# One factor for the second softmax's sum and the RMS norm, taken from turned squares

## The chip, the core and the metric

The kernel runs on one core of a Trainium2 chip. A core has TensorE (PE in the profile) for matrix products, VectorE (DVE), ScalarE (ACT), GpSimd (POOL), and a queue engine SP that issues the DMAs. The metric is the device time of one launch in microseconds (us).

## The reference, cut to what matters

Two softmax attentions come first, for 8 batches, 8 heads, 576 tokens and a head dimension of 64; 32 packed queries per head gather the tokens, and the tokens then read the packed rows back:

```
p_packed = sm_attn(p, k, v)                # 32 rows a head
out      = sm_attn(q, p_packed, p_packed)  # 576 tokens, softmax over 32 weights
x        = out, 8 heads side by side       # 4608 tokens x 512
xn       = x / sqrt(mean(x*x) + 1e-6) * rms_g
h        = silu(xn @ w_gate) * (xn @ w_val)
```

Four products with further weights follow (`w_out`, `w1`, `w2`, `w3`, `w_out2`). The change touches the second softmax and the RMS norm.

## The kernel before, in words

The kernel never forms `x`. It multiplies the packed rows with the gate and value weights (`wb_unit`, L383 to L397), and a dense stage multiplies that with the second softmax's weights of one batch, laid out as `ah` and `al`, the two halves of a split float32 (`split`, L58: ScalarE writes the high part, VectorE subtracts). `ah[:, e]` and `al[:, e]` exist for e = 0 and 1, four heads each.

`dense_units` (L418) runs over 8 batches and 6 column groups; each pair makes 8 units of six 288-column products. One unit after the other, even units (gate) are read by ScalarE's tanh (L438) and then VectorE (L439, "th"), odd ones (value) by ScalarE's copy (L447) and GpSimd (L448); in batch 0 VectorE does that last step (L444). Four PSUM banks hold the units, so unit n+4 can't start before unit n has been read. The six products of a unit take, in order, `ah` 0, `ah` 1, `al` 0, `al` 1, `ah` 0, `ah` 1. After units 3, 11, 19, 27, 35 and 43 of a batch stands the next `wb_unit`: one product (L391), a ScalarE copy (`wbh`) and a VectorE subtraction (`wbl`).

All engines run their instructions in program order, and the order is written out by hand. `unpack(b)` (L284) is a generator of 18 steps, `pack(b)` (L202) one of 7, and `ow` converts weights (two ScalarE, two VectorE, one GpSimd instruction each). `planned` (L490) takes a step of a generator after a unit: `UNPACK`, `PACK` and `WOUT` hold, for the batches 2 to 6, the unit within the batch (0 to 47) after which each step is issued; `PLAN` does so for batches 0 and 1 (units 0 to 95), and a string of letters for the prologue (x is a filler product, p, u, P, U are steps of pack and unpack). While batch b runs in the dense stage, `unpack(b+1)` is issued between its units.

The 18 steps of `unpack` before, for a batch other than 0: 1 scores (L303) and VectorE's 32x32 transposes; 2 to 5 row maximum, subtraction, exp; 6 and 7 row sum, reciprocal `rs2`, and GpSimd's multiplication of `a2` by it (L322); 8 and 9 the transposes into `a2T` (L327), with a DMA that rotates half 1 into `turned`; 10 and 11 the product of `a2T` with the 32x32 Gram matrix `G` (L343) and the elementwise product `sq`; 12 GpSimd's addition of the two halves of `sq` (L352); 13 five products with a column of ones (L359), which sum over heads, and `ssq` (L361); 14 GpSimd's power of -0.5 (L364); 15 five TensorE transposes that spread the factor over all partitions (L369) and VectorE's multiplication of half 0 (L371); 16 the same multiplication for half 1; 17 and 18 the splits into `ah` and `al`. Small PSUM results use `slot("at")`, of which there are two.

Of the kernel before, what the change touches and what calls it, by code (L numbers as in the profile page):

```python
# [8 lines left out]
F32 = mybir.dt.float32  # L9
# [23 lines left out]
def packed_attention_swiglu_bilinear(ctx: ExitStack, tc, qT, kT, v, v_end, pT, rms_g, w_gv, w_out,  # L33
                                     w1, w2, w3T, w_out2, out):
    nc = tc.nc
# [16 lines left out]
    def slot(tag):  # L52
        return slots.tile([128, 2, 512], F32, tag=tag, name=tag, bufs=2)
# [15 lines left out]
    att = att_ctx.enter_context(tc.tile_pool(name="att", bufs=1, side="left"))  # L69
# [23 lines left out]
    def load_q(b):  # L93
        load("q", qT, b, 2)
# [90 lines left out]
    wgv = wraw.tile([128, NC, 2, DFF], F32, name="wgv")  # L185
    bdP1T = att.tile([128, 2, NC, 2, NP], F32, name="bdP1T")
    G = att.tile([128, 2, 2, NP], F32, name="G")
    mhalf = att.tile([128, R], F32, name="mhalf")
    ones = att.tile([128, 2], F32, name="ones")
    nc.gpsimd.memset(ones, 1.0 / DM)  # L190
    nc.scalar.activation(out=ones[:, 1:], in_=ones[:, :1], func=AF.Exp)
    nc.gpsimd.memset(ones, 1.0 / DM)
    nc.gpsimd.memset(mhalf, -0.5)
    nc.gpsimd.memset(bdP1T, 0.0)


# [2 lines left out]
    def place(c, e):  # L199
        return 32 * ((c + e) % NC)  # L200
# [80 lines left out]
    NB = S // 32  # L281


    def unpack(b):  # L284
        assert ("bd", b) in over
        qs = raw.pop(("q", b))
        a2 = att.tile([128, 2, NB, NP], F32, tag="a2", name="a2")
        mx2 = att.tile([128, 2, NB], F32, tag="mx2", name="mx2")
        rs2 = att.tile([128, 2, NB], F32, tag="rs2", name="rs2")

        def halves(x):
            return x.rearrange("p (a n) -> p a n", a=2)
# [13 lines left out]
        for a, t in enumerate(ts):
            nc.vector.transpose(out=a2.rearrange("p e t n -> p e (t n)")[:, :, HALF * a:HALF * a + HALF],
                                in_=t[:, :, :HALF])
        yield
        if b > 1:  # L310
            load_q(b + 2)
        for e in range(2):
            nc.vector.tensor_reduce(out=mx2[:, e], in_=a2[:, e], axis=AX.X, op=ALU.max)
            yield
            nc.vector.tensor_tensor(out=a2[:, e], in0=a2[:, e], in1=wide(mx2[:, e]), op=ALU.subtract)
            nc.scalar.activation(out=a2[:, e], in_=a2[:, e], func=AF.Exp, scale=SCALE)
            yield
        for e in range(2):
            nc.vector.tensor_reduce(out=rs2[:, e], in_=a2[:, e], axis=AX.X, op=ALU.add)
            nc.vector.tensor_scalar(out=rs2[:, e], in0=rs2[:, e], scalar1=1e-9, scalar2=None, op0=ALU.add)  # L320
            nc.vector.reciprocal(out=rs2[:, e], in_=rs2[:, e])
            nc.gpsimd.tensor_tensor(out=a2[:, e], in0=a2[:, e], in1=wide(rs2[:, e]), op=ALU.mult)  # L322
            yield
        a2T = att.tile([128, 2, S], F32, tag="a2T", name="a2T")
        order = (0, 1) if b == 0 else (1, 0)
        for e in order:
            nc.vector.transpose(out=a2T[:, e], in_=a2[:, e].rearrange("p t n -> p (t n)"))  # L327
            if b and e:
                turned = att.tile([128, S], F32, tag="turned", name="turned")
                nc.sync.dma_start(out=turned[:96], in_=a2T[32:, 1])  # L330
                nc.sync.dma_start(out=turned[96:], in_=a2T[:32, 1])
            yield

        assert ("made", b) in over
        sq = att.tile([128, 2, S], F32, tag="sq", name="sq")
        ts = [slot("at") for _ in range(2)]
        for a in range(2):
            for e in range(2):
                for c in range(NC):
                    r = place(c, e)  # L340
                    k = r if b == 0 else 32 * c
                    x = turned[k:k + 32] if b and e else a2T[k:k + 32, e]
                    nc.tensor.matmul(ts[e][r:r + 32, a, :HALF], lhsT=G[k:k + 32, b % 2, e],  # L343
                                     rhs=x[:, HALF * a:HALF * a + HALF],
                                     start=True, stop=True, tile_position=(k, r))
        over.add(("G", b))
        for e in range(2):
            nc.vector.tensor_tensor(out=halves(sq[:, e]), in0=ts[e][:, :, :HALF], in1=halves(a2T[:, e]),
                                    op=ALU.mult)
            yield  # L350
        if b:
            nc.gpsimd.tensor_tensor(out=sq[:, 0], in0=sq[:, 0], in1=sq[:, 1], op=ALU.add)  # L352
        yield
        ssq = att.tile([128, R], F32, tag="ssq", name="ssq")
        rinv = att.tile([128, R], F32, tag="rinv", name="rinv")
        t = slot("at")
        for r in range(R):
            for e in range(1 if b else 2):
                nc.tensor.matmul(t[:, 0, 2 * r:2 * r + 2], lhsT=sq[:, e, T0[r]:T0[r] + 128], rhs=ones,  # L359
                                 start=(e == 0), stop=(e == 1 or b > 0), skip_group_check=True)  # L360
        nc.vector.tensor_scalar(out=ssq, in0=t[:, 0, :2 * R].rearrange("p (r j) -> p r j", j=2)[:, :, 0],  # L361
                                scalar1=0.0, scalar2=1e-6, op0=ALU.max, op1=ALU.add)
        yield
        nc.gpsimd.tensor_tensor(out=rinv, in0=ssq, in1=mhalf, op=ALU.pow)  # L364
        yield

        t = slot("at").rearrange("p a n -> p (a n)")
        for r in range(R):
            nc.tensor.transpose(t[:, 64 + T0[r]:192 + T0[r]], rinv[:, r:r + 1].to_broadcast([128, 128]), ident)  # L369
        for e in range(2):  # L370
            nc.vector.tensor_tensor(out=a2T[:, e], in0=a2T[:, e], in1=t[:, 64:64 + S], op=ALU.mult)  # L371
            yield
        ah = dp.tile([128, 2, S], F32R, tag="ah", name="ah", bufs=2)
        al = dp.tile([128, 2, S], F32R, tag="al", name="al", bufs=2)
        res["a2n", b] = (ah, al)
        for e in range(2):
            split(ah[:, e], al[:, e], a2T[:, e], nc.vector)
            yield

# [134 lines left out]
    for n in range(16):  # L514
        r, c = GROUPS[n // 4]
# [9 lines left out]

    gens = dict(x=spin(), p=pack(0), u=unpack(0), c=gvw, d=gvd, w=wb_first(), l=later(), P=pack(1), U=unpack(1),
                Q=pack(2), V=unpack(2), R=pack(3), o=ow)
    for x in ("pxxpxdxcxppdpcdpccdxcuduudcxuldupuxcuuw"
              "xxxxxdxlcuxxxxxxdcuuduuuPxlPPluPuxuuPldP"):
        next(gens[x], None)  # L530
    for x in "pu":
        drain(gens[x])
    PLAN = [("P", [22]),
# [585 lines left out]
```

## Time and the profile before

| | us |
|---|---|
| Median of 3 runs | 1346.66 (1344.73 to 1348.36) |
| Profiled execution, its own time | 1344.77 |
| Its span in the trace | 1342.9 |
| TensorE busy | 1321.9 (98%) |
| VectorE busy | 876.5 (65%) |
| ScalarE busy | 577.4 (43%) |
| GpSimd busy | 556.0 (41%) |

The granted TensorE clock is 0.996 on the mean. The dense stage with the attention in it ends at 482.6 us; what follows is not touched by the change. Busy shares are means over stages with different limits; a TensorE that counts as busy may still be pipelining.

### The profile page before, as it was taken

The page shows a single profiled execution, that of the slowest core. Times are in us where ns is not written, and L with a number is a line of the kernel's source. Part 1 is how long each engine was busy: PE and PEld are TensorE (multiplying, and loading weights), DVE is VectorE, ACT ScalarE, POOL GpSimd, SP SyncE. Part 2 cuts the span into 40 slices and gives each one's busy share as a digit, 9 for nine tenths or more (in the row PEclk, how much of TensorE's full clock was granted, in tenths as well). Part 3 has the DMA queues.
Part 4 walks back from the last instruction along what each step waited for, and adds up shares of the span by engine and source line. Part 5 has one row for each costly group of instructions (what it writes and reads, how often), then busy time and mean ns, then how long its engine had stood idle before and what let it go on. Part 6 is the DMA issues. An engine that isn't in the chain of part 4 may idle for free.

```text
span 1342.9 us, 23644 instructions
## 1 busy us (share of the span) xinstructions
PE 1321.9 (98%) x9010; PEld 1123.7 (84%) x9010; DVE 876.5 (65%) x1286; ACT 577.4 (43%) x1117; POOL 556.0 (41%) x467
## 2 busy tenths in 40 slices
PE   7989999999999999999999999999999999999998
PEld 6768788888888888888888888888888888899998
DVE  5796677777777557726474664578559657657645
ACT  5545566666666655525243442134015104305113
POOL 3341546656556542203221313455346335435442
PEclk9989999999999999999999999999999999999999
DMA  9855467647442576724399885656665755787775
GB/s 343 308 187 203 161 211 255 225 148 266 131 154 106 165 250 217 246 76 163 106 379 390 311 284 212 215 212 230 256 207 203 281 188 217 252 297 264 282 273 184
DMA packets 88706, 304.04 MB, mean 226 GB/s; under 512 B 9872, under 2 KB 14992, under 8 KB 74384
## 3 DMA queue, kind: packets, MB, share of 16 engines
q1 hardware_dynamic: 88592, 302.52, 63.9%
q8 instruction: 71, 1.16, 0.4%
q14 instruction: 43, 0.35, 0.1%
HBM read 223.87 MB, written 76.55 MB: 224 GB/s over the span
## 4 chain that ended last, share of the span: by engine, by line
PE 90%; DVE 6%; DMA 1%; issue 1%; ACT 1%; POOL 0%; SPq 0%; DVEq 0%; ACTq 0%; POOLq 0%
PE gv L432 22%; PE at L636 15%; PE gv L946 13%; PE at L946 13%; PE gv L636 7%; PE at L1035 5%; PE gv L1035 5%; PE at L391 3%; PE gv L736 3%; DVE sl L60 1%; DMA w<-in_w_gv_dram 1%; DVE wbl L60 1%; PE at L359 1%; PE at L343 1%; DVE wgv L121 1%
## 5 line engine op out<-in xcount | busy, mean ns | idle before, releaser
L448 POOL TENSOR_TENSOR ht<-th,vl 128x288 f32<-128x288 f32 x168 | 138.6, 834 | 122.1 <-ACT vl L447 67.8
L432 PE MATMUL gv<-ah,wbh 128*128 128x288 f32 x768 | 174.4, 308 | 4.1 <-DVE th L439 3.7
L432 PEld LDWEIGHTS gv<-ah,wbh 128*128 128x128 f32 x768 | 121.2, 188 | 55.1 <-issue 22.5
L432 PE MATMUL gv<-al,wbh 128*128 128x288 f32 x768 | 164.6, 295 | 0.0
L432 PE MATMUL gv<-ah,wbl 128*128 128x288 f32 x768 | 164.1, 295 | 0.0
L60 DVE TENSOR_TENSOR hl<-hr,hh 128x512 fp32r<-128x512 f32 x108 | 100.2, 933 | 72.8 <-ACT hh L59 69.2
L972 POOL TENSOR_TENSOR s<-uc 128x512 f32<-128x512 f32 (+1 forms) x40 | 48.9, 1222 | 231.7 <-DVE uc L928 231.7
L946 PE MATMUL gv<-xh,w 128*128 128x512 f32 (+1 forms) x560 | 137.7, 367 | 0.0
L946 PE MATMUL at<-xh,w 128*128 128x512 f32 (+1 forms) x560 | 137.7, 367 | 0.0
L123 POOL TENSOR_TENSOR c_o<-c_o,c_y 128x512 int32<-128x512 int32 x52 | 70.7, 1360 | 146.5 <-DVE c_o L121 123.3
L439 DVE SCALAR_TENSOR_TENSOR th<-th,gv 128x288 f32<-128x288 f32 x192 | 85.0, 446 | 62.3 <-ACT th L438 51.9
L432 PEld LDWEIGHTS gv<-al,wbh 128*128 128x128 f32 x768 | 123.4, 188 | 0.0
L432 PEld LDWEIGHTS gv<-ah,wbl 128*128 128x128 f32 x768 | 123.2, 188 | 0.0
L59 ACT ACTIVATE hh<-hr 128x512 fp32r<-128x512 f32 x108 | 67.4, 629 | 113.6 <-PE at L636 55.8
L946 PEld LDWEIGHTS gv<-xh,w 128*128 128x128 f32 x560 | 102.5, 188 | 13.3
L946 PEld LDWEIGHTS at<-xh,w 128*128 128x128 f32 x560 | 102.5, 188 | 13.2
L636 PE MATMUL at<-hh,wo_l 128*128 128x512 f32 x288 | 112.1, 389 | 0.0
L636 PE MATMUL at<-hl,wo_h 128*128 128x512 f32 x288 | 112.1, 389 | 0.0
L636 PE MATMUL at<-hh,wo_h 128*128 128x512 f32 x288 | 112.0, 389 | 0.0
L438 ACT ACTIVATE th<-gv 128x288 f32<-128x288 f32 x192 | 78.8, 410 | 53.6 <-PE gv L432 52.1
L447 ACT ACTIVATE vl<-gv 128x288 f32<-128x288 f32 x168 | 69.1, 411 | 50.2 <-PE gv L432 36.5
L60 POOL TENSOR_TENSOR xl<-yi,xh 128x1024 fp32r<-128x1024 f32 (+1 forms) x20 | 56.6, 2837 | 74.9 <-ACT xh L59 74.4
(164 smaller groups left out, 2837.9 us busy)
## 6 DMA issues: line engine op xcount, KB each, us to landing
w<-ws_d SPq DMA_DIRECT2D x40, 1024.0 KB, 5.1
w<-w_d SPq DMA_DIRECT2D x35, 1024.0 KB, 4.8
w<-ws_d SPq DMA_DIRECT2D x40, 768.0 KB, 4.9
hT_d<-ht SPq DMA_DIRECT2D x96, 288.0 KB, 3.4
hr<-hT_d SPq DMA_DIRECT2D x108, 256.0 KB, 4.9
w<-in_w_gv_dram SPq DMA_DIRECT2D x24, 512.0 KB, 6.1
w<-in_w_out_dram SPq DMA_DIRECT2D x20, 512.0 KB, 5.5
q<-in_qT_dram SPq DMA_DIRECT2D x8, 1152.0 KB, 7.4
```

What stands on the lines that cost most here:

```text
L59: nc.scalar.activation(out=hi, in_=src, func=AF.Copy)
L60: eng_lo.tensor_tensor(out=lo, in0=src, in1=hi.bitcast(F32), op=ALU.subtract)
L123: nc.gpsimd.tensor_tensor(out=d, in0=d, in1=shape(y), op=ALU.add)
L432: nc.tensor.matmul(t[:, :HALF], lhsT=w[:, e, 256 * i + 128 * f:256 * i + 128 * f + 128], rhs=x[:, e, HALF * hf:HALF * hf + HALF], start=(n ...
L438: nc.scalar.activation(out=th, in_=t[:, :HALF], func=AF.Tanh, scale=0.5)
L439: nc.vector.scalar_tensor_tensor(out=th, in0=th, scalar=1.0, in1=t[:, :HALF], op0=ALU.add, op1=ALU.mult)
L447: nc.scalar.activation(out=vl, in_=t[:, :HALF], func=AF.Copy, scale=0.5)
L448: nc.gpsimd.tensor_tensor(out=ht[:, hf], in0=th, in1=vl, op=ALU.mult)
L636: nc.tensor.matmul(acc[m], lhsT=w[:, kk, 128 * m:128 * m + 128], rhs=x, start=(kk == 0 and a == 0), stop=(kk == NF - 1 and a == 2))
L946: nc.tensor.matmul(t, lhsT=wi[:, r, pos, a], rhs=x[:, j, r, :w], start=(start and at == 0), stop=(at == 5), skip_group_check=True)
L972: nc.gpsimd.tensor_tensor(out=s2, in0=u2, in1=c22, op=ALU.mult)
L1035: nc.tensor.matmul(acc[m][BANK[j]], lhsT=wi[:, s, k, 128 * m:128 * m + 128], rhs=x, start=(j in (0, 5, 4, 3) and k == 0 and n == 0), stop= ...
```

## The change

For batch 0 everything stays. For the other batches, step 6 and 7 no longer multiply `a2` by `rs2`: the weights stay unnormalised. Step 12 turns both halves of `sq` back (two more VectorE transposes, into `a2T`), sums them per token and head in one reduction over 2x576 elements, multiplies twice by `rs2` and adds the halves. Step 13 is one product with a block identity `heads`, which sums over the heads and gives the sum to all partitions. Step 14 raises it to -0.5 (18 columns in place of 5) and multiplies `rs2` by it. Steps 15 and 16 multiply `a2` by that factor on GpSimd, and steps 17 and 18 each begin with another transpose into `a2T`. `heads` is built once with three VectorE instructions. The prologue's string and all the plans have new numbers.

```diff
+    heads = att.tile([128, NC, NP], F32, name="heads")
+    nc.vector.tensor_reduce(out=heads[:, 0], in_=ident.rearrange("p (c t) -> p t c", c=NC), axis=AX.X, op=ALU.add)
+    nc.vector.tensor_scalar(out=heads[:, 0], in0=heads[:, 0], scalar1=1.0 / DM, scalar2=None, op0=ALU.mult)
+    nc.vector.tensor_copy(heads[:, 1:], heads[:, :1].to_broadcast([128, NC - 1, NP]))
...
-            nc.gpsimd.tensor_tensor(out=a2[:, e], in0=a2[:, e], in1=wide(rs2[:, e]), op=ALU.mult)
+            if b == 0:
+                nc.gpsimd.tensor_tensor(out=a2[:, e], in0=a2[:, e], in1=wide(rs2[:, e]), op=ALU.mult)
...
+        def turn(e, src=a2):
+            nc.vector.transpose(out=a2T[:, e], in_=src[:, e].rearrange("p t n -> p (t n)"))
...
-        if b:
-            nc.gpsimd.tensor_tensor(out=sq[:, 0], in0=sq[:, 0], in1=sq[:, 1], op=ALU.add)
...
+        else:
+            part = mx2
+            both = att.tile([128, NB], F32, tag="both", name="both")
+            turn(0, sq.rearrange("p e (t n) -> p e t n", n=NP))
+            turn(1, sq.rearrange("p e (t n) -> p e t n", n=NP))
+            nc.vector.tensor_reduce(out=part, in_=a2T.rearrange("p e (t n) -> p e t n", n=NP), axis=AX.X, op=ALU.add)
+            for _ in range(2):
+                nc.vector.tensor_tensor(out=part, in0=part, in1=rs2, op=ALU.mult)
+            nc.vector.tensor_tensor(out=both, in0=part[:, 0], in1=part[:, 1], op=ALU.add)
+            yield
+            t = slot("at")
+            nc.tensor.matmul(t[:, 0, :NB], lhsT=heads.rearrange("p c t -> p (c t)"), rhs=both, start=True, stop=True)
+            nc.vector.tensor_scalar(out=both, in0=t[:, 0, :NB], scalar1=0.0, scalar2=1e-6, op0=ALU.max, op1=ALU.add)
+            yield
+            nc.gpsimd.tensor_tensor(out=both, in0=both, in1=mhalf, op=ALU.pow)
+            nc.vector.tensor_tensor(out=rs2, in0=rs2, in1=both[:, None, :].to_broadcast([128, 2, NB]), op=ALU.mult)
+            yield
+            for e in range(2):
+                nc.gpsimd.tensor_tensor(out=a2[:, e], in0=a2[:, e], in1=wide(rs2[:, e]), op=ALU.mult)
+                yield
...
         for e in range(2):
+            if b:
+                turn(e)
             split(ah[:, e], al[:, e], a2T[:, e], nc.vector)
...
-    for x in ("pxxpxdxcxppdpcdpccdxcuduudcxuldupuxcuuw"
-              "xxxxxdxlcuxxxxxxdcuuduuuPxlPPluPuxuuPldP"):
+    for x in ("xxxppdpxcxdpxcpdpcdxccuxducduuxdpxuuulxu"
+              "wxdcxxxlcuxxxxdxcxxuuduuuPxPPluuuPudPlllP"):
...
-            ("U", [13, 15, 15, 16, 17, 18, 19, 20, 21, 24, 25, 28, 32, 34, 42, 42, 43, 45]),
+            ("U", [13, 15, 15, 16, 17, 18, 19, 20, 21, 24, 25, 29, 33, 36, 42, 42, 43, 44]),
...
-            ("V", [63, 64, 67, 68, 72, 72, 73, 76, 79, 81, 82, 82, 84, 84, 87, 89, 91, 94]),
-            ("R", [78, 78, 82, 89, 90, 92, 94]),
+            ("V", [59, 63, 64, 67, 71, 71, 73, 75, 78, 80, 80, 81, 83, 84, 88, 89, 91, 94]),
+            ("R", [78, 78, 89, 91, 92, 94, 95]),
...
-    UNPACK = [-1, -1, 0, 2, 7, 8, 12, 16, 16, 23, 24, 25, 30, 30, 35, 36, 38, 43]
-    PACK = [6, 6, 13, 27, 28, 30, 47]
-    WOUT = [18, 22, 25, 28, 33, 37]
+    UNPACK = [0, 0, 3, 6, 7, 7, 8, 11, 12, 18, 18, 18, 22, 24, 25, 39, 39, 45]
+    PACK = [6, 6, 19, 27, 35, 37, 39]
+    WOUT = [14, 19, 30, 34, 37, 46]
```

In `PLAN`, U and V are `unpack(1)` and `unpack(2)`, and R is `pack(3)`. Its other lists (weight conversions c and d, loads l, `ow`) are shifted by some units as well.

## Rows read from the trace of the kernel before

**Rows 1.** Busy time by stretch: us, then PE, PEld, DVE, ACT, POOL; PEclk.

```profile
51.00:100.00 49.00, 43.55 (x387) 33.86 (x387) 45.42 (x87) 29.10 (x55) 23.16 (x18) 0.93 0.71 252
...
259.30:313.60 54.30, 54.19 (x606) 44.98 (x603) 40.53 (x71) 35.88 (x81) 32.25 (x35) 1.00 0.58 203
```

**Rows 2.** TensorE's timeline in a regular batch: start, us, instruction.

```profile
207.54 1.25 PE L359 MATMUL at<-ones,sq 128*128 128x2 f32 x10
208.65 0.51 PE L432 MATMUL gv<-ah,wbh 128*128 128x288 f32 x2
...
212.71 0.71 PE L369 MATMUL at<-ident,rinv 128*128 128x128 f32 x5
213.35 1.09 PE L391 MATMUL at<-wgv,gP1T 64*32 64x512 f32 x16
```

**Rows 3.** Groups by line and form: busy us, mean ns of one.

```profile
L348 DVE TENSOR_TENSOR sq<-at,a2T 128x576 f32<-128x576 f32 x16 | 11.9, 751 | 0.3 <-PE at L343 0.3
...
L319 DVE TENSOR_REDUCE rs<-a 128x18 f32<-128x576 f32 x16 | 11.8, 740 | 0.0
L371 DVE TENSOR_TENSOR a2T<-a2T,at 128x576 f32<-128x576 f32 x16 | 11.8, 749 | 2.4 <-PE at L369 2.4
L327 DVE STREAM_TRANSPOSE a2T<-a 128x576 f32<-128x576 f32 x16 | 11.7, 757 | 0.0
...
L352 POOL TENSOR_TENSOR sq<-sq 128x576 f32<-128x576 f32 x7 | 10.9, 1555 | 2.0 <-DVE rs L231 2.0
...
L364 POOL TENSOR_TENSOR rinv<-ssq,mhalf 128x5 f32<-128x5 f32 x8 | 9.4, 1180 | 0.3 <-DVE ssq L361 0.2
...
L320 DVE TENSOR_SCALAR rs<-rs 128x18 f32<-128x18 f32 x16 | 4.3, 271 | 0.5
...
L361 DVE TENSOR_SCALAR ssq<-at 128x5 f32<-128x5 f32 x8 | 1.3, 158 | 1.2 <-PE at L359 1.2
```

**Rows 4.** Instructions on the tile a2T: ns least, median, most.

```profile
L59 ACT ACTIVATE ah<-a2T x16: 670/678/699, 49.1 to 434.4; 128x576 fp32r<-128x576 f32 x16
L60 DVE TENSOR_TENSOR al<-a2T,ah x16: 751/990/1759, 49.8 to 435.1; 128x576 fp32r<-128x576 f32 x16
```

**Rows 5.** Timeline of all engines around one wb_unit, units 4 to 6 behind it.

```profile
284.41 1.09 PE L391 MATMUL at<-wgv,gP1T 64*32 64x512 f32 x16
...
285.43 0.54 PE L432 MATMUL gv<-ah,wbh 128*128 128x288 f32 x2
...
285.61 1.03 ACT L59 ACTIVATE wbh<-at 128x1024 fp32r<-128x1024 f32 x1 [0.18 <-PE at L391]
...
286.67 1.23 DVE L60 TENSOR_TENSOR wbl<-at,wbh 128x1024 fp32r<-128x1024 f32 x1 [0.32 <-ACT wbh L59]
...
287.81 0.45 DVE L439 SCALAR_TENSOR_TENSOR th<-th,gv 128x288 f32<-128x288 f32 x1
...
288.01 1.20 PE L214 MATMUL at<-k,pTs 64*32 64x288 f32 x32
```

**Rows 6.** The chain that ended last: start, us, what.

```profile
115.56 1.09 PE at L230 x10
...
306.84 1.13 PE at L343 x32
```

**Rows 7.** VectorE's timeline in the next regular batch.

```profile
301.00 1.43 DVE L327 STREAM_TRANSPOSE a2T<-a 128x576 f32<-128x576 f32 x2
...
302.71 0.43 DVE L120 TENSOR_SCALAR c_t<-c_h 128x512 int32<-128x512 int32 x1
303.17 0.69 DVE L121 SCALAR_TENSOR_TENSOR c_o<-c_h,c_t 128x512 int32<-128x512 int32 x1
...
308.16 0.75 DVE L348 TENSOR_TENSOR sq<-at,a2T 128x576 f32<-128x576 f32 x1
```

**Rows 8.** Short stretches of batch 0, columns as in Rows 1.

```profile
74.00:82.00 8.00, 4.82 (x41) 3.97 (x40) 7.79 (x17) 4.40 (x9) 3.62 (x4) 0.91 0.01 2
82.00:90.00 8.00, 6.95 (x66) 4.38 (x67) 7.51 (x14) 4.32 (x8) 4.09 (x3) 0.67 0.88 291
```

**Rows 9.** VectorE's first instruction, in the timeline.

```profile
9.20 0.76 DVE L218 TENSOR_REDUCE mx<-at 128x1 f32<-128x576 f32 x1 [9.20 <-PE at L214]
```

More of the change, by code (lines that the diff above doesn't have):

```diff
@@ L187, in packed_attention_swiglu_bilinear @@
     G = att.tile([128, 2, 2, NP], F32, name="G")
-    mhalf = att.tile([128, R], F32, name="mhalf")
+    mhalf = att.tile([128, S // 32], F32, name="mhalf")
     ones = att.tile([128, 2], F32, name="ones")
@@ L321, in unpack @@
             nc.vector.reciprocal(out=rs2[:, e], in_=rs2[:, e])
-            nc.gpsimd.tensor_tensor(out=a2[:, e], in0=a2[:, e], in1=wide(rs2[:, e]), op=ALU.mult)
+            if b == 0:
+                nc.gpsimd.tensor_tensor(out=a2[:, e], in0=a2[:, e], in1=wide(rs2[:, e]), op=ALU.mult)
             yield
         a2T = att.tile([128, 2, S], F32, tag="a2T", name="a2T")
-        order = (0, 1) if b == 0 else (1, 0)
-        for e in order:
-            nc.vector.transpose(out=a2T[:, e], in_=a2[:, e].rearrange("p t n -> p (t n)"))
+        def turn(e, src=a2):
+            nc.vector.transpose(out=a2T[:, e], in_=src[:, e].rearrange("p t n -> p (t n)"))
+        for e in (0, 1) if b == 0 else (1, 0):
+            turn(e)
             if b and e:
@@ L350, in unpack @@
             yield
-        if b:
-            nc.gpsimd.tensor_tensor(out=sq[:, 0], in0=sq[:, 0], in1=sq[:, 1], op=ALU.add)
[L353 to L371, printed above, removed]
-            yield
+        if b == 0:
+            ssq = att.tile([128, R], F32, tag="ssq", name="ssq")
+            rinv = att.tile([128, R], F32, tag="rinv", name="rinv")
+            yield
+            t = slot("at")
+            for r in range(R):
+                for e in range(2):
+                    nc.tensor.matmul(t[:, 0, 2 * r:2 * r + 2], lhsT=sq[:, e, T0[r]:T0[r] + 128], rhs=ones,
+                                     start=(e == 0), stop=(e == 1), skip_group_check=True)
+            nc.vector.tensor_scalar(out=ssq, in0=t[:, 0, :2 * R].rearrange("p (r j) -> p r j", j=2)[:, :, 0],
+                                    scalar1=0.0, scalar2=1e-6, op0=ALU.max, op1=ALU.add)
+            yield
+            nc.gpsimd.tensor_tensor(out=rinv, in0=ssq, in1=mhalf[:, :R], op=ALU.pow)
+            yield
+            t = slot("at").rearrange("p a n -> p (a n)")
+            for r in range(R):
+                nc.tensor.transpose(t[:, 64 + T0[r]:192 + T0[r]], rinv[:, r:r + 1].to_broadcast([128, 128]), ident)
+            for e in range(2):
+                nc.vector.tensor_tensor(out=a2T[:, e], in0=a2T[:, e], in1=t[:, 64:64 + S], op=ALU.mult)
+                yield
[9 more added lines that the diff above has]
+            yield
+            t = slot("at")
+            nc.tensor.matmul(t[:, 0, :NB], lhsT=heads.rearrange("p c t -> p (c t)"), rhs=both, start=True, stop=True)
+            nc.vector.tensor_scalar(out=both, in0=t[:, 0, :NB], scalar1=0.0, scalar2=1e-6, op0=ALU.max, op1=ALU.add)
+            yield
+            nc.gpsimd.tensor_tensor(out=both, in0=both, in1=mhalf, op=ALU.pow)
+            nc.vector.tensor_tensor(out=rs2, in0=rs2, in1=both[:, None, :].to_broadcast([128, 2, NB]), op=ALU.mult)
+            yield
+            for e in range(2):
+                nc.gpsimd.tensor_tensor(out=a2[:, e], in0=a2[:, e], in1=wide(rs2[:, e]), op=ALU.mult)
+                yield
@@ L376, in unpack @@
         for e in range(2):
+            if b:
+                turn(e)
             split(ah[:, e], al[:, e], a2T[:, e], nc.vector)
@@ L532, in packed_attention_swiglu_bilinear @@
         drain(gens[x])
-    PLAN = [("P", [22]),
[8 rows of a table removed]
-    UNPACK = [-1, -1, 0, 2, 7, 8, 12, 16, 16, 23, 24, 25, 30, 30, 35, 36, 38, 43]
-    PACK = [6, 6, 13, 27, 28, 30, 47]
-    WOUT = [18, 22, 25, 28, 33, 37]
+    PLAN = [("P", [23]),
[8 rows of a table added]
+    UNPACK = [0, 0, 3, 6, 7, 7, 8, 11, 12, 18, 18, 18, 22, 24, 25, 39, 39, 45]
+    PACK = [6, 6, 19, 27, 35, 37, 39]
+    WOUT = [14, 19, 30, 34, 37, 46]
     steps = [(at, gens[x]) for x, at in PLAN]
```

10 rows, old and new, of the table PLAN are left out of this document.

## The prediction

> **What bounds the kernel now.** I read the busy time by stretch first. In a regular batch of the dense stage (three alike, one shown) TensorE is busy 54.19 of 54.30 us at the full clock, and VectorE 40.53: TensorE sets the time there, and VectorE has a quarter of it free [rows 1]. In batch 0 it is the other way round: from 51 to 100 us VectorE is busy 45.42 of 49 us and TensorE 43.55, because weight conversions, L444 and `unpack(1)` all fall on VectorE. The chain that ended last then says the same: in the regular batches it goes from product to product on TensorE, in batch 0 it hops between VectorE instructions. So an instruction taken from TensorE is worth its own time in batches 1 to 6, if VectorE, which gets the work instead, never makes TensorE wait. Last I read the timelines around the points where the new plan puts its steps, since every engine goes in program order and a wait is decided by what stands ahead in each queue.
>
> **What TensorE is relieved of.** The five products with ones (ten records, float32 takes two each) hold TensorE from 207.54 to the next unit at 208.65, 1.11 us; the five transposes from 212.71 to 213.35, 0.64 us [rows 2]. One product with `heads` is two such records: a fifth of 1.11, 0.22 us. Saved: 1.53 us a batch, for seven batches **10.7 us**. That is the whole possible gain, 0.8%.
>
> **What the other engines get.** VectorE: four more transposes of 128x576 (0.757 us each), one reduction of 128x1152 (not in the trace; above the 0.74 us of 128x576 and at most twice it, taken as 1.4 because the other 576-wide groups scale with their elements), four small instructions (0.158 to 0.271 us, taken as 0.2), less two multiplications of 0.749 [rows 3]. Net some 3.7 us a batch, so 44 of 53 us. As a sum that fits; the question is where it stands. GpSimd loses the addition of `sq` (1.555 us) and its two multiplications by `rs2` only move. Its power grows from 5 to 18 columns. Nothing in the trace is 18 wide: below, the 1.18 us of 5 columns; above, 18/5 of it, 4.2 us; I take 3.8, since nearly all of a five-column instruction of 1.18 us must be the power itself when 128x576 of addition takes 1.555 [rows 3]. The Trainium skill (GPSIMD Engine Reference, 3.1 Elementwise) counts some 2.6 cycles an element for GpSimd's two-input arithmetic; by an estimate from it 13 more columns would add 0.03 us, and the power would stay at 1.2 us. The row speaks against that, and the sum is the same with either while the hold is covered.
>
> VectorE's multiplication of `rs2` stands right behind the power (step 14, unit 24) and holds VectorE while it runs; queued behind it is unit 26's th instruction, whose PSUM bank unit 30 needs. Four units, a `wb_unit` and L245 lie between, over 5 us, so a hold of 3.8 is covered; with less cover each microsecond too much costs one per batch. The `turned` DMAs are issued seven units ahead of their product in both plans, and no longer behind GpSimd's multiplication: nothing. The three instructions for `heads` come when VectorE is idle until 9.20 us [rows 9]: nothing. The loads moved (q of batch 2 into the prologue, k and q of batch 3 to units 46 and 51) still stand a batch ahead of use. The prologue's string has the same conversions in another order and 23 fillers for 22: nothing, within 2 us either way.
>
> **Place one: the edge of a batch.** Step 18 now comes after unit 45, has a transpose ahead of its split, and stands behind `wbl` of unit 43's `wb_unit` and unit 44's th. Before, it came at 43, ahead of that `wbl`, and L303 (units -1) stood between the batches; now L303 is after unit 0 and covers nothing. I count from the start of that `wb_unit`'s product. TensorE: the next unit 1.02 later (285.43 less 284.41), units of 0.86 (three up to 288.01) [rows 5]; the new batch starts at 4.46, its fourth product, the first that reads `al` 1, at 4.89. VectorE: `wbl` starts at 2.26, th at 3.40 (287.81) and lasts 0.45 [rows 5], to 3.85; transpose 0.757 [rows 3], 4.6; `ah` 0.678, 5.3; `al` 0.990, 6.27 [rows 4]. Lost: 6.27 less 4.89, **1.4 us** a batch, 1.15 with the shortest `al` (0.751) and 2.15 with the longest (1.759). The longest `al` rows lie beside GpSimd's work. The Trainium skill (GPSIMD Engine Reference, 1. Specifications) says that GpSimd shares its SBUF interfaces with VectorE, with contention where VectorE reads two SBUF inputs; the spread of the `al` rows from 0.751 to 1.759 us agrees, and if every such edge had GpSimd beside it, by the rule the loss would be 2.15 and the sum 4 us higher.
>
> **Place two: units 18 to 24.** Steps 10, 11 and 12 are all issued after unit 18, and after unit 19 a pack step, a conversion and a `wb_unit`. From the start of L343: TensorE has 1.13, unit 19, L230's 1.09 [rows 6], `wb_unit` 1.02, three units, 0.22, unit 23; unit 24 could start at 7.8. It needs unit 20's bank, read by a th behind all of this on VectorE: `sq` starts at 1.32 (308.16 less 306.84) [rows 6, 7], two of them 1.43 as two transposes are [rows 7], two transposes to 4.2, the reduction to 5.6, three small to 6.2 (`heads` is due at 6.7: no wait there), two small of the pack to 6.6, the conversion's pair to 7.75, `wbl` to 8.9 (1.14 from start to start), th to 9.35. That is 1.6 late, 1.0 if neighbours overlap as transposes do by 0.08; I take **1.2 us**. With a reduction as short as 0.74 it is 0.4.
>
> **Batches 0 and 1** have own plans. In batch 1 (V) step 12 comes at 81 and `heads` at 83: due three units after L343's 1.13, at 3.7, ready at 6.2: 2.3 lost after overlaps. At its edge step 17 stands at 91 ahead of `wbl`, step 18 at 94: the same count gives 2.0. In batch 0, L214 at unit 46 gives TensorE a microsecond more and the edge costs 0.6; step 12 (3.4 us on a VectorE that has hardly any gap) has four units up to `heads`: I take 1.0, bounds 0 and 3.4.
>
> **Sum.** -10.7 + 5 x (1.4 + 1.2) + 2.3 + 2.0 + 0.6 + 1.0 = +8.2 us. On the profiled execution's own 1344.77 us that is 1353.0. It lies 1.9 below the median of the runs; I split that and say **1354**.
>
> **Rivals.**
> - *VectorE keeps ahead (faster).* TensorE is late anyway at both places, or ScalarE and VectorE run their short instructions closer than I count; then the 10.7 us are kept, less up to 2 for batch 0: about 1336. It decides at the edge: `al` 1 done 4.9 us after the `wb_unit`'s product. For it: before, TensorE waits almost nowhere in a regular batch, with 40 us of VectorE work. Against: step 18 hangs behind th of unit 44 and four serial instructions, each with a row. 0.15.
> - *Only the edges cost.* The reduction is short and conversions slip in: place two and V's step 12 cost nothing: 1344.8 - 10.7 + 7 + 3.6, near 1345, 1346 against the median. No measurable change. 0.20.
> - *The power holds VectorE.* It starts late behind unit 21's and 23's GpSimd work and a conversion's, or takes over 5 us; th of unit 26 is late and 30 waits, say 1.2 more in five batches: 1360. For it: 32 us of other work on GpSimd a batch [rows 1]. 0.13.
> - *Batch 0 or the clock.* VectorE's extra 3.4 us there count in full, and a TensorE pause lowers the clock again: in 74 to 82 us TensorE was busy 4.82 of 8, and in the next 8 us the granted clock fell to 0.67 [rows 8], that is half speed (1.2 for 2.4 GHz) for part of it. Four to seven us more: 1360. 0.07.
> - The forecast keeps 0.45, with 1349 to 1359 as its own range.
>
> **How the numbers follow.** About 0.3%, 4 us, is what measuring can tell from no change. Slower: the forecast less 0.06 that reaches below 1350.7, and the two dear rivals, 0.59. Same: 0.20 + 0.06. Faster: 0.15. For 8 in 10 the range goes from 1340 (half of the gain kept) to 1363.
>
> **What would show it.** In the new trace: no L359 or L369 after batch 0, a `heads` product of about 0.22 us; unit 0's second and fourth product waiting for `ah` and `al`, near 1.4 us in all; unit 24 waiting for th; the regular batch some 55.4 us from L343 to L343, not 52.8. If TensorE's idle time stays at a few tenths per batch, places one and two are wrong; if the power is 1.2 us, its scaling is; if batch 0 or the prologue moves by over 3 us, the taken 1.0 and nothing are.

## The result and the profile after

The changed kernel takes **1357.12 us** (median of four, 1356.27 to 1360.04), the kernel before beside it 1347.51 (1344.73 to 1348.83): 1.008 times as long, 95% interval 1.0068 to 1.0093. Forecast were 1354 and a range of 1340 to 1363. The profiled execution shown is the longest of the four (own time 1360.04, span 1358.3), that of before nearly the shortest of its runs (1344.77, span 1342.9), so the traces lie 15.4 us apart and the medians 9.6.

Each batch has six groups of eight units, with one `wb_unit` product in each. From the start of the first such product of a batch (it stands behind unit 3) to that of the next makes a table without gaps, worked out from TensorE's timelines. "Start" is where the first one stands:

```
                       start  batch0 batch1  batch2 batch3 batch4 batch5 batch6
before                 54.35  64.28  57.16   54.30  54.32  54.32  54.30  48.46
after                  56.40  68.55  61.92   54.87  54.88  54.89  54.87  50.73
e1 old lists           54.40  69.24  59.37   58.63  58.60  58.60  58.65  49.34
e3 edge early          54.92  67.90  60.39   55.72  57.01  55.71  57.04  50.42
e4 V early             53.81  67.86  63.76   54.87  54.87  54.87  54.87  50.73
e5 cover back          55.02  69.22  65.04   53.53  55.06  55.04  55.06  51.76
e6 rs2 on GpSimd       55.78  69.12  60.38   54.87  54.93  54.87  54.87  49.76
e7 e1 + rs2 on GpSimd  57.31  70.64  59.05   59.25  59.99  59.36  60.01  48.77
e8 e7 + turn early     57.46  67.82  62.00   57.53  57.50  58.71  57.52  48.54
e9 old lists, 0 and 1  56.68  69.63  62.87   54.85  54.94  54.88  54.86  50.71
e10 e1, 5-wide power   57.32  70.28  57.35   56.65  57.89  57.92  56.59  48.31
e11 5-wide power       54.21  68.47  60.40   54.87  54.87  54.86  54.85  49.74
e12 heads later        53.45  68.03  61.12   54.87  54.86  54.88  54.87  50.71
e13 turns, edge early  54.79  67.05  61.17   54.03  54.02  54.01  54.00  48.25
```

What follows the last column is alike, 901.1 to 901.9 us, in all. "Regular" are batches 2 to 5; they repeat to 0.1 us between kernels that have the same code there (after, e4, e9, e12). The start doesn't: seven kernels whose code is after's up to there (e3 to e6, e11 to e13) have 53.45 to 55.78, so its 2.05 us between the two traces are no finding, and batches 0 and 1 carry some of that spread. Between the traces the 15.4 us are 2.05 of start, 4.27 and 4.76 in batches 0 and 1, 2.27 in the four regular batches, 2.27 in batch 6.

Busy time by stretch, of after (columns as in [rows 1], which hold the same batch 0 stretch and a regular batch of before):

```profile
51.00:100.00 49.00, 40.94 (x393) 32.59 (x381) 46.38 (x84) 29.20 (x56) 16.70 (x13) 0.90 0.70 237
262.15:317.03 54.88, 53.78 (x597) 44.08 (x589) 42.49 (x78) 36.51 (x82) 32.89 (x33) 1.00 0.64 217
```

In the regular batch TensorE is busy 0.41 us less than before, though the batch is 0.57 longer: it now waits. VectorE is busy 1.96 us more (42.49 for 40.53). The groups of after (busy us, mean ns | idle before), which answer to [rows 3]:

```profile
L332 DVE STREAM_TRANSPOSE a2T<-a 128x576 f32<-128x576 f32 x30 | 23.0, 767 | 0.0
L393 POOL TENSOR_TENSOR both<-both,mhalf 128x18 f32<-128x18 f32 x7 | 22.5, 3218 | 0.0
...
L332 DVE STREAM_TRANSPOSE a2T<-sq 128x576 f32<-128x576 f32 x14 | 10.0, 752 | 0.0
...
L384 DVE TENSOR_REDUCE mx<-a2T 128x36 f32<-128x1152 f32 x7 | 9.5, 1354 | 0.2
...
L394 DVE TENSOR_TENSOR rs<-rs,both 128x36 f32<-128x36 f32 x7 | 4.3, 616 | 18.4 <-POOL both L393 18.4
```

The reduction takes 1.354 us (taken: 1.4), the power 3.218 (taken: 3.8). VectorE stands still for 18.4 us in all for the power. What TensorE waited for, from 55 to 190 us (batches 0 and 1) and then, below the dots, from 190 to 500 us (total, times, longest). In the second stretch the view of the kernel before lists no wait at all:

```profile
PE at L390 <- DVE both L387: 4.1, 2, 2.2
PE gv L460 <- DVE th L467: 2.7, 3, 1.3
PE at L351 <- ACT G L281: 2.1, 1, 2.1
PE at L278 <- ACT bdP1T L266: 1.7, 1, 1.7
...
PE gv L460 <- ACT ah L59: 3.5, 5, 0.7
PE gv L460 <- DVE al L60: 1.3, 5, 0.3
```

**Place one, the edge.** Timelines of TensorE, VectorE and ScalarE after the last `wb_unit` of a batch, which answer to [rows 5]:

```profile
287.23 0.53 PE L460 MATMUL gv<-ah,wbh 128*128 128x288 f32 x2
...
291.51 0.40 PE L460 MATMUL gv<-ah,wbh 128*128 128x288 f32 x1 [0.71 <-ACT ah L59]
...
292.31 0.40 PE L460 MATMUL gv<-al,wbh 128*128 128x288 f32 x1 [0.26 <-DVE al L60]
...
292.90 1.20 PE L307 MATMUL at<-q,bdP1T 64*32 64x288 f32 x32
```

```profile
288.47 1.23 DVE L60 TENSOR_TENSOR wbl<-at,wbh 128x1024 fp32r<-128x1024 f32 x1 [0.75 <-ACT wbh L59]
289.61 0.44 DVE L467 SCALAR_TENSOR_TENSOR th<-th,gv 128x288 f32<-128x288 f32 x1
289.97 0.77 DVE L332 STREAM_TRANSPOSE a2T<-a 128x576 f32<-128x576 f32 x1
291.49 0.76 DVE L60 TENSOR_TENSOR al<-a2T,ah 128x576 fp32r<-128x576 f32 x1 [0.75 <-ACT ah L59]
```

```profile
290.78 0.68 ACT L59 ACTIVATE ah<-a2T 128x576 fp32r<-128x576 f32 x1 [1.19 <-DVE a2T L332]
```

The chain is the forecast's, link by link: `wbl`, th, transpose, `ah`, `al`. From 287.23 to 292.90 five units take 5.67 us. Four undisturbed units take 3.37 in these traces, so five would take 4.22: 1.45 lost.

**Place two, units 18 to 24.** TensorE and VectorE of the same batch, which answer to [rows 6, 7]:

```profile
312.64 0.45 PE L351 MATMUL at<-a2T,G 32*32 32x288 f32 x4
...
314.70 1.43 PE L234 MATMUL at<-ident,e 128*128 128x128 f32 x10
...
319.77 0.29 PE L390 MATMUL at<-both,heads 128*128 128x18 f32 x2
...
320.79 0.43 PE L460 MATMUL gv<-ah,wbh 128*128 128x288 f32 x2
...
321.60 0.53 PE L460 MATMUL gv<-ah,wbh 128*128 128x288 f32 x2
```

```profile
318.53 0.18 DVE L387 TENSOR_TENSOR both<-mx 128x18 f32<-128x18 f32 x1
...
319.95 1.22 DVE L60 TENSOR_TENSOR wbl<-at,wbh 128x1024 fp32r<-128x1024 f32 x1
321.08 0.81 DVE L467 SCALAR_TENSOR_TENSOR th<-th,gv 128x288 f32<-128x288 f32 x2
```

VectorE is as late as counted: th of unit 20 starts 8.4 us after L351 and ends at 8.9 (forecast 9.35). But unit 24 starts at 320.79, before that th has even begun. So it doesn't need unit 20's bank. Of units 20 to 23 only unit 21 had been read by then, in ScalarE's timeline:

```profile
319.23 0.41 ACT L475 ACTIVATE vl<-gv 128x288 f32<-128x288 f32 x1
```

Unit 24 therefore has unit 21's bank. Unit 25 starts at 321.60, just behind the end of unit 20's th near 321.53, and by that has unit 20's. So the rule of the section on the kernel, that unit n+4 can't start before unit n has been read, doesn't hold here. Nothing is lost.

### The profile page after: what moved, and what is told of

It reads as the page before. It is cut to its first block, busy times and chain, and to the rows that moved or that the text cites. A ratio compares the mean times of both kernels' runs of the same rounds, so it can differ in the third digit from the quotient of the medians.

```text
span 1358.3 us, 23464 instructions
## 1 busy us (share of the span) xinstructions
PE 1326.5 (98%) x8927; PEld 1124.4 (83%) x8927; DVE 892.7 (66%) x1338; ACT 580.1 (43%) x1117; POOL 561.4 (41%) x460
## 4 chain that ended last, share of the span: by engine, by line
PE 85%; DVE 5%; ACT 1%; issue 1%; POOL 0%; DVEq 0%; ACTq 0%; POOLq 0%
PE gv L460 19%; PE at L664 14%; PE gv L974 13%; PE at L974 13%; PE gv L664 7%; PE at L1063 5%; PE gv L1063 5%; PE gv L764 3%; PE at L419 3%; DVE sl L60 1%; DVE a2T L332 1%; PE at L307 0%; DVE xl L60 0%; DVE th L467 0%; PE at L249 0%
## 5 line engine op out<-in xcount | busy, mean ns | idle before, releaser
L476 POOL TENSOR_TENSOR ht<-th,vl 128x288 f32<-128x288 f32 x168 | 137.3, 825 | 120.6 <-ACT vl L475 56.3
```

Source lines behind the costliest of these rows:

```text
L476: nc.gpsimd.tensor_tensor(out=ht[:, hf], in0=th, in1=vl, op=ALU.mult)
```

## The experiments

**e1 and what it undid.** The new arithmetic with the string and all lists of before:

```diff
-    UNPACK = [0, 0, 3, 6, 7, 7, 8, 11, 12, 18, 18, 18, 22, 24, 25, 39, 39, 45]
-    PACK = [6, 6, 19, 27, 35, 37, 39]
+    UNPACK = [-1, -1, 0, 2, 7, 8, 12, 16, 16, 23, 24, 25, 30, 30, 35, 36, 38, 43]
+    PACK = [6, 6, 13, 27, 28, 30, 47]
...
```

> The changed arithmetic of unpack, with the prologue string and all plan lists of the kernel before. Theory A (the loss is in where the new plan puts the steps, the new arithmetic itself is a gain): regular batch near 52.9 us against 54.3 before and 54.9 after, because step 18 at unit 43 stands ahead of wbl and L307 covers the edge; batches 0 and 1 still lose 2 to 5 us, since the longer chain of step 12 has no more room there; time 1338 to 1344, faster than before. Theory B (VectorE with 44 us of work a batch and the power of 3.2 us are too much wherever the steps stand): a regular batch at or above 54.3 us, time 1347 or more.

1372.89 us, 1.0189 times before (1.0168 to 1.021). Of a gain there is nothing: theory A, that only the new positions cost, falls. The regular batch takes 58.6 us, 4.3 more than before. The timeline of e1 where it begins (engines mixed, in order of time), then short stretches (columns as in [rows 1]):

```profile
277.78 3.22 POOL L393 TENSOR_TENSOR both<-both,mhalf 128x18 f32<-128x18 f32 x1
...
281.03 0.77 DVE L394 TENSOR_TENSOR rs<-rs,both 128x36 f32<-128x36 f32 x1 [4.84 <-POOL both L393]
281.73 0.44 DVE L467 SCALAR_TENSOR_TENSOR th<-th,gv 128x288 f32<-128x288 f32 x1
...
281.79 0.41 ACT L475 ACTIVATE vl<-gv 128x288 f32<-128x288 f32 x1 [2.06 <-POOL ht L476]
...
282.22 0.54 PE L460 MATMUL gv<-ah,wbh 128*128 128x288 f32 x2 [1.84 <-DVE th L467]
...
288.83 0.68 ACT L59 ACTIVATE ah<-a2T 128x576 fp32r<-128x576 f32 x1 [3.59 <-DVE a2T L332]
```

```profile
279.00:281.00 2.00, 1.38 (x14) 0.83 (x6) 0.00 (x0) 0.72 (x2) 2.00 (x2) 1.00 1.01 401
281.00:283.00 2.00, 0.78 (x6) 0.78 (x7) 1.93 (x4) 1.22 (x3) 1.45 (x2) 1.00 0.96 350
283.00:285.00 2.00, 2.00 (x12) 2.00 (x11) 2.00 (x3) 2.00 (x6) 1.32 (x2) 0.56 0.38 141
```

Under the old positions the power comes right behind other GpSimd work. VectorE does nothing from 277 to 281 us, th comes late, TensorE stops for 1.84 us, and in the stretch behind the stop the granted clock is 0.56, so some of it ran at the lower of its two levels (1.2 instead of 2.4 GHz). Two more holds are in the rows: ScalarE's vl waits for GpSimd, and its copy of ah waits 3.59 us for the new transpose with vl queued behind it. The old lists don't suit the new arithmetic; e7, e8 and e10 take the holds one by one.

**e3, the edge moved forward alone.**

```diff
-    UNPACK = [0, 0, 3, 6, 7, 7, 8, 11, 12, 18, 18, 18, 22, 24, 25, 39, 39, 45]
+    UNPACK = [0, 0, 3, 6, 7, 7, 8, 11, 12, 18, 18, 18, 22, 24, 25, 27, 36, 41]
```

> The changed kernel with only the last three entries of UNPACK moved: 27, 36, 41 for 39, 39, 45 (batches 2 to 6). Theory A: the 1.4 us that unit 0 of the next batch waits for ah and al go, nothing takes their place; five batches, some 7 us, time near 1350, regular batch 53.5 us. Theory B: VectorE has no room, the wait comes back at other units (a th or wbl late), time 1354 to 1358.

A miss, dearer than either theory: 1361.97 us, 1.0113 (1.0093 to 1.0133). The waits at the edge are gone, and another stands in their place, in ScalarE's and TensorE's timelines and in short stretches of e3:

```profile
280.45 0.68 ACT L59 ACTIVATE ah<-a2T 128x576 fp32r<-128x576 f32 x1 [2.04 <-DVE a2T L332]
281.04 0.39 ACT L475 ACTIVATE vl<-gv 128x288 f32<-128x288 f32 x1
281.33 0.56 ACT L266 ACTIVATE bdP1T<-at 64x128 f32<-64x128 f32 x2
```

```profile
281.64 0.56 PE L278 MATMUL at<-bdP1T 64*32 64x32 f32 x16 [1.78 <-ACT bdP1T L266]
```

```profile
280.00:282.00 2.00, 0.33 (x14) 0.22 (x16) 1.25 (x3) 1.50 (x5) 0.53 (x2) 1.00 1.00 387
282.00:284.00 2.00, 2.00 (x19) 1.96 (x20) 1.56 (x4) 1.98 (x6) 0.68 (x2) 0.79 0.31 119
284.00:286.00 2.00, 2.00 (x10) 2.00 (x9) 1.28 (x3) 1.13 (x4) 2.00 (x3) 0.50 0.04 12
286.00:288.00 2.00, 2.00 (x22) 1.04 (x21) 1.38 (x2) 0.98 (x3) 0.88 (x2) 0.86 0.73 268
```

The ah copy is issued with its transpose, which stands on VectorE behind a conversion and `wbl`. ScalarE waits with it, the copy of bdP1T waits behind, and TensorE wants that for L278. Then the four units behind take 4.90 instead of 3.37 us, in stretches with a granted clock of 0.79, 0.50 and 0.86: the wait of 1.78 us costs 1.5 more.

**e4 and e5, V earlier; the batch's first step over the edge.**

```diff
-            ("V", [59, 63, 64, 67, 71, 71, 73, 75, 78, 80, 80, 81, 83, 84, 88, 89, 91, 94]),
+            ("V", [59, 60, 61, 64, 68, 68, 70, 72, 75, 77, 77, 78, 83, 84, 88, 89, 91, 94]),   # e4
...
-    UNPACK = [0, 0, 3, ...
+    UNPACK = [-1, -1, 3, ...   # e5
```

(e4 has the last of Q at 74 for 75 besides.)

> The changed kernel with only batch 1 touched: steps 2 to 12 of unpack(2) three units earlier (60 to 78 for 63 to 81), the last step of pack(2) at 74 for 75; heads stays at unit 83. Theory A: the wait of heads for both (2.2 us in batch 1) goes, edge unchanged, time about 2 us less, near 1355. Theory B: VectorE is late before it, the wait only moves, time unchanged within 1 us.

1360.41 us, 1.0101 (1.0082 to 1.012), a miss: in batch 1 the wait for `both` (2.24 us) is gone, and TensorE waits 3.7 us for ScalarE's vl instead; the batch is 63.76 for 61.92.

> The changed kernel with only the first two entries of UNPACK moved from 0, 0 to -1, -1 (batches 2 to 6): the scores L307 stand between the batches again. The splits end when they did. Theory A: TensorE has 1.13 us of other work while it would wait, so of the 1.4 us at each edge some 1.1 go, time 5 us less, near 1352. Theory B: the loss is VectorE's, which gets nothing from this: 1356 to 1358.

1358.17 us, 1.0088 (1.0065 to 1.011), a miss for theory A, and no different from after. In batch 2 L307 covers the edge: TensorE waits for nothing there, and the batch takes 53.53 us, 1.34 less than in after, with these two positions alone changed. But from batch 3 on L218 waits up to 1.1 us for `wbl` (3.4 us in three times between 240 and 460 us), and a batch takes 55.06; batch 1 has 65.04 for 61.92.

**e6, the root multiplied in by GpSimd.** One word of L394, in the changed kernel:

```diff
-            nc.vector.tensor_tensor(out=rs2, in0=rs2, in1=both[:, None, :]...
+            nc.gpsimd.tensor_tensor(out=rs2, in0=rs2, in1=both[:, None, :]...
```

> The changed kernel with one word changed: the multiplication of the softmax factors by the root (128x2x18) is made by GpSimd behind its own power, no longer by VectorE. Theory H (the wait of VectorE for the power costs time): the 18.4 us of VectorE's waits for L393 go; in the regular batch they were hidden (no idle time of TensorE stands behind them), so it stays at 54.9 us; batch 0, batch 1 and the last batch lose up to 1 us each less: 1354 to 1356. Rival P (the waits that set the end are those at the edge, behind ScalarE's copy of ah and the heads product; VectorE's wait for the power is idle time that is covered everywhere): no change within 0.1%, 1356 to 1358.

1357.03 us, 1.0078 (1.0062 to 1.0094): the rival's value. VectorE no longer waits for L393, and TensorE's waits at the edges of e6 are those of after, to the tenth (`ah` 3.5 us and `al` 1.3, five times each). Only batch 6 is shorter beyond the spread, 49.76 for 50.73. Those 18.4 us of VectorE were covered, as forecast, but for about one.

**e7 and e8, the old lists with the holds taken away.** e7 is e1 with e6's word. e8 is e7 with each transpose a step ahead of its copy:

```diff
             for e in range(2):
                 nc.gpsimd.tensor_tensor(out=a2[:, e], in0=a2[:, e], in1=wide(rs2[:, e]), op=ALU.mult)
+                if e:
+                    turn(0)
                 yield
...
-            if b:
-                turn(e)
+            if b and e == 0:
+                turn(1)
             split(ah[:, e], al[:, e], a2T[:, e], nc.vector)
```

> The new arithmetic under the old prologue order and the old step lists (which took 58.6 us for a regular batch, 1372.9 in all), with the multiplication by the root on GpSimd instead of VectorE. Theory H: the loss began where VectorE waited 4.84 us for GpSimd's power at step 14 and TensorE then waited 1.84 us for a tanh product of VectorE's; without that wait the regular batch returns to 54 to 55 us and the time to 1346 to 1352. Rival T: the loss is that of the new transpose ahead of ScalarE's copy of ah (step 17), with the clock that falls behind it; then the regular batch stays above 56.5 us and the time above 1360.

1376.26 us, 1.0216 (1.0199 to 1.0233). Theory H falls: a regular batch got longer by 0.6 to 1.4 us. VectorE no longer waits for the power, but GpSimd's queue carries the multiplication too. Between 190 and 460 us TensorE's waits for th fall from 11.5 us in e1 to 8.3, and those for ScalarE's vl, which itself waits for GpSimd's ht, rise from 3.2 to 7.8.

> As the kernel before it (old step lists, root multiplied in by GpSimd), and each new transpose of the weights issued a step earlier than its copy (the first at the end of step 16, the second at the start of step 17), so that ScalarE's copy of ah finds its transpose done. Theory T: 1.5 to 3.5 us per regular batch come back against the kernel before it, and the time falls to 1340 to 1350. Theory H: within 2 us of the kernel before it; slower by some us if the transposes now hold VectorE for GpSimd's multiplication.

1366.75 us, 1.0152 (1.0134 to 1.017): 9.5 us less than e7, some 0.6 to 2.5 a regular batch. Theory T holds for its part, not for the whole: the time lies far above its 1340 to 1350, and e8 stays at 57.5 to 58.7 a regular batch. TensorE still waits for vl behind GpSimd (6.2 us in four times between 240 and 350 us).

**e9, the old lists for batches 0 and 1 alone**, string and PLAN of before, UNPACK, PACK and WOUT of after:

> The changed kernel with the old prologue order and the old list for batches 0 and 1, and the new lists from batch 2 on. If what the prologue (+2.0 us) and batches 0 and 1 (+4.3 and +4.8) lost is the new positions' doing, some 6 us of the 11 come back: 1349 to 1353. If it is the arithmetic's (VectorE's extra transposes, the power, the heads product, wherever they stand), the start loses as much as before or more: 1355 to 1362. The regular batch stays at 54.9 us either way.

1360.97 us, 1.0105 (1.009 to 1.012), inside the second case's range. Batch 0 takes 69.63 us, and 67.82 to 70.64 in the other four kernels with the old lists: its loss isn't the new positions'. Of batch 1 (62.87) e9 doesn't show that. Up to its edge it goes as in e1, within 0.1 us. There e1 has L307 ahead of the new batch (the -1 of the old UNPACK), while in e9 TensorE waits 0.81 us for `ah`, the granted clock falls to 0.50, and the batch ends 3.5 us later. With the old lists throughout, e1, e7 and e10 have batch 1 at 57.35 to 59.37, against 60.38 to 61.92 where the new lists stand unchanged there (after, e3, e6, e11). e8, with the turns early, has 62.00. So the positions at that edge bear part of batch 1's loss.

**e10 and e11, a power of 5 columns** under the old and the new lists. Both leave the root out of the other 13 columns, so their output isn't the reference's and only their time is of use:

```diff
-            nc.gpsimd.tensor_tensor(out=both, in0=both, in1=mhalf, op=ALU.pow)
+            nc.gpsimd.tensor_tensor(out=both[:, :5], in0=both[:, :5], in1=mhalf[:, :5], op=ALU.pow)
```

> The new arithmetic under the old order and step lists (1372.9 us, regular batch 58.6), with the power of batches 1 to 7 taken of the first 5 of 18 columns alone (the width that it has in the kernel before); the other 13 columns keep the value without the root. Theory G (the 3.2 us power stands in GpSimd's queue ahead of the products ht, ScalarE's copy vl waits for its buffer, and the banks come free late; moving the multiplication by the root to GpSimd therefore made nothing better): the power falls to about 1.2 us, and 2 to 4 us of each regular batch come back: 55 to 56.5 us, 1352 to 1360 in all. Rival T (the transposes ahead of ScalarE's copy of ah): the regular batch stays above 57.5 us, the time above 1366.

1362.73 us, 1.0108 (1.0091 to 1.0125): 0.7 to 2.1 us of each regular batch come back, 10 in all against e1. Theory G has its part, but the time lies between the two theories' ranges and the 55 to 56.5 isn't reached (56.59 to 57.92). Groups of e10:

```profile
L393 POOL TENSOR_TENSOR both<-both,mhalf 128x5 f32<-128x5 f32 x7 | 8.2, 1168 | 0.0
L394 DVE TENSOR_TENSOR rs<-rs,both 128x36 f32<-128x36 f32 x7 | 4.9, 700 | 14.7 <-POOL both L393 14.7
```

> The changed kernel with the power taken of 5 of the 18 columns, the rest left without the root. Theory C (the new lists cover the power in the regular batch, where VectorE's wait for it ends before TensorE needs anything): regular batch 54.9 us as before within 0.1; batches 0 and 1 and the last lose up to 2 us less together; 1354.5 to 1357. Rival G: the power holds GpSimd there too: 1348 to 1353, with a regular batch of 53.5 to 54.2.

1357.33 us, 1.0073 (1.0058 to 1.0088): no change, theory C, whose regular batch of 54.9 it has. The power's length costs 5.4 us in batches 2 to 5 under the old lists and nothing under the new.

**e12, the heads product of batches 0 and 1 later.**

```diff
-            ("U", [..., 29, 33, 36, 42, 42, 43, 44]),
+            ("U", [..., 29, 35, 36, 42, 42, 43, 44]),
-            ("V", [..., 81, 83, 84, 88, 89, 91, 94]),
+            ("V", [..., 81, 85, 86, 88, 89, 91, 94]),
```

> The changed kernel with the heads product of batches 0 and 1 two units later (units 35 and 85 for 33 and 83; the power of batch 1 at 86 for 84), so that VectorE's two transposes and sum are done when TensorE comes to it (it waited 1.90 and 2.24 us). If these waits are a loss of their own: 3 to 5 us come back, with the clock that falls behind them: 1352 to 1354. If VectorE is the late engine there and the wait turns up behind another of its results (a tanh product, the transposes of step 17): 1356 to 1360.

1357.39 us, 1.0075 (1.006 to 1.009): no change. TensorE's waits in batches 0 and 1 of e12:

```profile
PE gv L460 <- DVE th L467: 4.5, 4, 2.2
PE at L351 <- ACT G L281: 2.1, 1, 2.1
PE at L278 <- ACT bdP1T L266: 1.9, 1, 1.9
```

The 4.1 us for `both` are gone; a th wait of 2.2, for VectorE again, stands in for part of them. That VectorE is late there whoever waits is the reading; where the rest of the 4.1 us goes isn't shown.

**e13, turns early and the edge early.** e6's word and e8's turns in the changed kernel, and

```diff
-            ("U", [..., 29, 33, 36, 42, 42, 43, 44]),
+            ("U", [..., 29, 35, 36, 40, 42, 43, 44]),
-            ("V", [..., 83, 84, 88, 89, 91, 94]),
+            ("V", [..., 83, 84, 87, 90, 92, 94]),
-    UNPACK = [..., 18, 18, 18, 22, 24, 25, 39, 39, 45]
+    UNPACK = [..., 18, 18, 18, 22, 24, 25, 33, 38, 43]
```

> The changed kernel with the root multiplied in by GpSimd, each transpose of the weights issued a step before its copy (as in the run under the old lists), and the last three steps of a batch at units 33, 38 and 43 for 39, 39 and 45 (batch 0: heads product at 35, first multiplication at 40; batch 1: last steps at 87, 90, 92, 94). If ScalarE's copy of ah, late at the edge of a batch and in front of the copies of P1 when it is moved forward alone, is what the changed kernel loses there, both waits go: the regular batch takes 53.2 to 53.8 us (1.1 to 1.7 less, below the 54.3 of the kernel before), and the time 1344 to 1351. If VectorE is the late engine whatever the order, a wait of 1.5 to 2.5 us turns up elsewhere in the batch, with a lower granted clock behind it: 55 to 57 us a batch, 1356 to 1365.

**1349.85 us** (eleven runs), 1.0019 times before (1.001 to 1.0028): 7 us better than after, 2 behind the kernel before. The regular batch takes 54.0 us, 0.3 less than before, though not the 53.2 to 53.8 expected; batch 6 48.25 for 48.46. TensorE's waits from 190 to 500 us:

```profile
PE gv L462 <- DVE th L469: 1.5, 4, 0.4
PE at L390 <- DVE both L387: 0.4, 1, 0.4
PE gv L462 <- DVE wbl L60: 0.3, 1, 0.3
```

No ah, no al, no bdP1T. So the edge of after was ScalarE's copy waiting for a transpose issued with it, and moving the pair apart and forward mends it where moving it forward alone (e3) only moved the wait. e13 changes three things in a regular batch; e6's word alone changes nothing there, but the turns early without the move forward were not run, so the two aren't priced apart.

## Why the prediction was right

The direction, the number and one of the two places held: 1354 said, 1357.1 measured, slower as forecast. By its steps:

- *Saved 1.53 us a batch.* L359 and L369 are gone from the unpacks of batches 1 to 7, and L390 fills 0.14 us in a regular batch (forecast 0.22). Not all of it arrives: from start to start L234 behind unit 19 takes 1.56 us where L230 took 1.34, and L218 1.41 where L214 took 1.13; the rows don't say why.
- *VectorE's 3.7 us more a batch:* the new instructions are about as long as taken, yet the regular stretch has only 1.96 more. The old ones take less: `al` and the conversions (L120, L121) take 9.2 us in it for 11.6. The sum didn't use the 3.7, so this cost it nothing.
- *Place one, 1.4 us:* 1.45, with the predicted chain; `al` took 0.76 us there and not the 0.990 taken, and the units ahead were 0.16 shorter than counted, two small errors that offset. Shown by e5's batch 2, where the edge is covered and the batch is 1.34 us shorter, and borne out by e13, where these waits are gone, the five units take 4.17 and a batch is 0.86 us shorter, with a new wait of 0.37 for th in it.
- *Place two, 1.2 us:* wrong. VectorE's times were near (8.9 for 9.35), the failed step is "It needs unit 20's bank". The banks don't go round strictly by four: unit 24 has unit 21's, and unit 20's goes to unit 25, a unit later. So the regular batch is 54.87 us, not the 55.4 forecast.
- *The power covered:* right, in length (3.218 for 3.8) and in cover (e6 and e11 change no regular batch), but for about 1 us in batch 6. e1 and e10 show what it costs without the cover. The Trainium skill (GPSIMD Engine Reference, 3.1 Elementwise) counts some 2.6 cycles an element for a two-input instruction; by an estimate from that rate the power would have stayed at 1.2 us. The row is 3.218, so the rate doesn't hold for a power.
- *Batch 1:* the wait for `heads` is 2.24 us (2.3). Its edge turned up as L278's 1.71 us wait for bdP1T behind the ah copy (2.0).
- *Batch 0, taken 0.6 and 1.0:* under-sized, and the prediction's own sign, over 3 us, says so. `heads` alone waits 1.90, and L351 2.15 for ScalarE's G (L343 waited 1.06 before, for another copy of ScalarE's). Short stretches of after, which answer to [rows 8]:

```profile
74.00:82.00 8.00, 5.20 (x56) 3.48 (x40) 7.83 (x17) 5.24 (x11) 2.56 (x2) 1.00 0.21 81
82.00:90.00 8.00, 5.37 (x44) 3.77 (x45) 7.90 (x15) 3.10 (x6) 3.39 (x3) 0.53 0.64 188
```

VectorE is full, TensorE pauses, and the clock falls to 0.53 (0.67 before). This is the rival *batch 0 or the clock*, which had 0.07: forecast were +0.07 us for batch 0 with its share of the saving and +2.77 for batch 1, the traces have +4.27 and +4.76 (e3, e6, e11, e12 and e13, with batch 1 between 60.38 and 61.17, would make the second +3.2 to +4.0). For batch 0 e9 and e12 show that neither the lists nor the place of `heads` decides it. Over the whole of batch 0 VectorE is busy 58.98 us for 55.67 before, and 58.6 to 59.1 in every kernel with the new arithmetic, whose batch 0 takes 67.05 to 70.64. That this load is the cause is argued from it, not shown by a run that takes it away.
- *The prologue, nothing within 2 us:* 2.05, and no finding, since the same code spreads over more than that. `heads` is built at 1.76 to 2.6 us, before VectorE has anything else to do.

So the sum came near partly by errors that offset. Batches 2 to 5 were forecast at +1.07 us each and have +0.57: place two gave back 1.2, the slower L218 and L234 took 0.5, and the other 0.2 is spread over the batch. Batches 0 and 1 have 6.2 us more than forecast in the traces, batch 6 1.2 more. That would be +13.6 without the start; the medians say +9.6, since the two profiled executions lie at opposite ends of their runs. How much of these 4 us belongs to batches 0 and 1 stays open.

## What to carry to other kernels

When work moves from the engine that is the bound to engines with room, add up not their busy time but what stands behind each new wait in their queues: here a copy issued together with the transpose that it needs blocked ScalarE's whole queue, and issuing the producer a step before its consumer gave 9.5 us back (e8 against e7), where shifting the steps alone cost some 5 (e3). A list of positions belongs to the instructions that it was made for: the same new code took 1372.9 us under the old lists and 1357.1 under the new, and 1349.9 with one multiplication on another engine, two transposes issued earlier and a list to suit them. Before counting a wait for a buffer, look up which earlier use the program gave that buffer to.

## What the runs showed of the hardware

- GpSimd's power goes by columns: 1.168 us for 128x5 (e10), 3.218 for 128x18, so by an estimate from the two 0.158 us a column and some 0.4 besides, while a whole 128x288 product (L476) took 0.80.
- A pause of TensorE of 1.84 us (e1) and one of 1.78 us (e3) were each followed by stretches with a granted clock of 0.50 to 0.58, which in e3 added 1.5 us to the pause; the waits of 0.71 and 0.26 us at after's edge were not, and its regular batch stayed at 1.00. In e9 waits of 1.10 and 0.81 us, 1.4 us apart, were followed by stretches at 0.55 and 0.50.
- The longest `al` fell from 1.759 us in before [rows 4] to 1.483, its median from 0.990 to 0.758, without a change to `al`. What runs beside it differs: of the 32 in the two traces, the 16 with no GpSimd instruction beside them took 0.751 to 0.759 us, and of the 16 with one, 15 took 0.886 to 1.759 and one 0.752. At after's edge there was none, so the dear case of place one, 2.15 us, didn't come.
